# Loading the query features of the layer below four slots sooner in the two sliding-window attention backwards

## The chip, the cores and the metric

The kernel runs on one core of a Trainium2 chip. The metric is the device time of one launch in microseconds (us), lower is better. The kernel before takes 2128.89 us, the median of 3 runs (2128.79 to 2133.01). The execution that the profiler recorded took 2126.94 us.

## The reference, cut to what matters

A sequence of 2048 rows with 640 features goes forward through four residual layers, and then the gradients of the input and of the four weight matrices are computed. Layers 0 and 2 are linear attention (A), layers 1 and 3 sliding-window softmax attention (B), all with 32 heads of 20 features.

```
phi = lambda t: where(t > 0, t + 1, exp(t)) + 1e-6
A:  q, k, v = split(x @ wqkv);  pq, pk = phi(q), phi(k)
    kv = einsum("bhsd,bhse->bhde", pk, v);  z = pk.sum(s)
    o = (pq @ kv) / (pq . z + 1e-6);  return o @ wo
B:  scores = q @ k.T / sqrt(20), kept where 0 <= i - j < 256
    o = softmax(scores) @ v;  return o @ wo
x = x + A(layernorm(x));  x = x + B(layernorm(x))      (twice)
out = x;  gradients of sum(out * grad_out) in x, A_wqkv, A_wo, B_wqkv, B_wo
```

The backward of a layer A needs, for all rows, the outer product of the query features `pq` with the gradient `dn` of numerator and denominator, summed over the whole sequence. These are the outer products of the title. They need the gradient that leaves the layer B above, and the gradients of keys and values need the finished sum.

## The kernel before, in words

The 2048 rows are 16 tiles of 128 rows, and two tiles make a chunk, so that there are eight chunks, c = 0 to 7. The passes run one after the other: forward through the four layers; attention backward of layer 3; linear attention backward of layer 2; attention backward of layer 1; the rest of that one; linear attention backward of layer 0 with the weight gradients.

An attention backward (`core`, L1433) goes through 24 visits per chunk (`core_visit`, L782). In a visit TensorE (PE in the profile) makes the products `dp` and `s` for two blocks of heads, ScalarE (ACT) the exponentials `e` (L811), GpSimd (POOL) masks them by affine selects (L826, L830), VectorE (DVE) multiplies `dp` by the `e` of three visits before into `ds` (L815). The `ds` of four visits before is turned: by TensorE into a PSUM tile named `flip` (L837), copied out to `dsT` by VectorE (L844) or ScalarE (L842), or in some visits by a transposing DMA. The products of six visits before are added up (`acc`).

Between these parts each visit carries pieces of other work from a written plan. `plan_before` (L909) prepares the next chunk: it loads `gb` and `ob`, and multiplies the turned gradient by `WoTB` into PSUM tiles named `dense`. `plan_behind` (L967) takes a finished chunk on to the layer below. The start of its plan is 32 slots per chunk, two chunks after the chunk itself; a slot is three quarters of a visit, so 32 slots are 24 visits. The places of its pieces within that are the list `bh` of `PLACES` (L53), the lists `bl3` and `bl1` for the last chunk:

- `load` (`bh[26]` = 3.9): the normalized rows `hnb` and the incoming gradient `gc`, 320 KB each; they are first used by `ln` (L1059, L1062) from slot 20.2 on.
- `turn`, `store`, the products `dh`, `ln`, `ln2`, `flip`, `prod`, `fold`, `red`: what makes the gradient of the layer below and from it `dn`.
- `load_q` (`bh[31]` = 38): the query features `pqb` of the chunk's two tiles, 320 KB, into a buffer of which there is one.
- `outer` (`bh[24]` = 40.2 and `bh[25]` = 44.6): three heads' groups each of the outer products `pqb` with `dn` into a PSUM tile named `outer`, added to `macc` by VectorE (L258).

With slot 38 a chunk's `pqb` load stands behind the `hnb` and `gc` loads of the next chunk, whose plan began at slot 32 of this one, so at 35.9. In layer 1 chunk 6 has its own places for some pieces (`late`, L1019), `load_q` among them. Plans are sorted by slot and handed out to half visits (`slots`, L903).

The PSUM tiles `flip`, `dense` and `outer` take turns in two buffers. During the attention backward the order on all five engines is the order in which the program issues the work, SyncE (SP) among them, and SyncE issues every DMA of the kernel (L148): its queue is one list, in which each entry waits for its own releases before the next can go. `put` (L153) and `tick` (L161) hold some of the DMAs back by parts of a visit; the loads of `plan_behind` are issued at their slot without that.

Of the kernel before, what the change touches and what calls it, by code (L numbers as in the profile page):

```python
# [49 lines left out]
    sp=[2.6, 1.1, -2.9, -3.4, 0.6, -3.8, 0.1, 0.4, 2, 1.8, 1.1, 0.8, 3, 1, 0.9, 0.5, 1.3, 1.1, 1, 1, 1.5],  # L50
    ms=[1, -0.2, 20, 31.2, 39.5],
    bf=[1.6, 4.2, 7.7, 10, 17.8, 7.7, 9.2, 10, 14, 28.4],
    bh=[13.4, 15.6, 15.8, 16.3, 17.5, 18.5, 20.2, 22.6, 25.2, 27.8, 30, 34.4, 18.7, 21.1, 21.1, 21.6, 23.8, 24.4, 25.1, 26, 29.6, 31.8, 33.3, 35.9, 40.2, 44.6, 3.9, 7.8, 7.5, 11.6, 20.7, 38],  # L53
    bl3=[13.4, 15, 15.5, 16.2, 17.3, 17.7, 18.5, 20.2, 25.9, 28.6, 29.3, 36, 19.7, 19.9, 20.3, 22.7, 23.9, 24.8, 26.3, 26.7, 30.1, 31.8, 33.1, 36.4, 40.2, 44.6, 13.4, -5.7, -4.4, 14, 19.4, 35.1],
    bl1=[12.9, 15.1, 15.5, 16.2, 18.1, 19.6, 20.2, 22.2, 25.7, 27.8, 30.7, 34.2, 18.7, 19.4, 21.1, 21.6, 23.4, 24.3, 24.3, 25.9, 29.6, 31, 33.3, 35.3, 40.9, 45, 0.5, -4.8, -3.6, -1.2, 0.5, 1],
    la=[-10.3, -2.5, 2.1, 2.4, 1.9, 3.2, 4.6, 6.2, 7.2, 8, 4.9, 8, 8.3, 10, 11.8, 13.9, 14, 16.2, 16.9, 17, 19.2, -2.3, 3.6],
# [1674 lines left out]
```

## Time and profile before

| | |
|---|---|
| median of 3 runs | 2128.89 us |
| profiled execution | 2126.94 us |
| span in the profile, first to last instruction | 2125.2 us |
| TensorE matmul busy | 1987.4 us, 94% of the span |
| VectorE, ScalarE, GpSimd busy | 1388.1, 1300.8, 1014.0 us |
| mean granted TensorE clock | 0.988 |
| attention backward of layer 3, about 660 to 1062 us | TensorE busy 372.64 of 402 us, DMA share 0.79 |
| attention backward of layer 1, about 1224 to 1626 us | TensorE busy 370.68 of 402 us, DMA share 0.77 |

In the timelines of this document a row gives the start in us from the start of the span, the duration in us, the engine (PE matmul, PEld weight load, SPq the queue that issues DMAs), the line, the operation, what it writes and reads, how many instructions were merged into the row, and in brackets the idle time of the engine before it with what ended it. A line 204 is the helper that issues every matmul, so those are told apart by their tiles.

### The profile page before, as it was taken

To read this page: it belongs to the slowest core of one execution; us is meant where nothing else is said; L and a number is where in the kernel's file an instruction comes from. 1 tells how busy PE (TensorE), PEld (TensorE's weight loads), DVE (VectorE), ACT (ScalarE), POOL (GpSimd) and SP (SyncE) were. 2 spreads that over 40 slices of the span, in tenths; PEclk is the share of its full clock that TensorE was granted. 3 is DMA by queue.
4 is the path that set the end of the run, shared out by engine and by line. 5 is a ranking of instruction groups with operands and counts; after the bars stand their busy time and mean duration, and the time that the engine had idled before them with its cause. 6 is when DMAs were issued, how large, how long until landed. Compare 5 with 4: busy or idle time off the path is not lost.

```text
span 2125.2 us, 75617 instructions
## 1 busy us (share of the span) xinstructions
PE 1987.4 (94%) x32332; PEld 1530.7 (72%) x32332; DVE 1388.1 (65%) x2696; ACT 1300.8 (61%) x1818; POOL 1014.0 (48%) x1594
## 2 busy tenths in 40 slices
PE   8989998899988899999979988999999899999999
PEld 6667776667766777777768777777777788887644
DVE  7788886788855888888848768888886244310000
ACT  6558888478886787777747767777776244420000
POOL 1046666056665577777633356777764312220000
PEclk9999999999999999999999999999999999999999
DMA  7598886688883688888899746889887989979650
GB/s 254 202 232 226 217 214 185 202 227 220 215 218 118 174 170 188 181 190 181 172 290 263 220 110 143 184 177 206 186 178 184 311 238 271 262 206 309 225 169 19
DMA packets 667937, 432.17 MB, mean 203 GB/s; under 512 B 396880, under 2 KB 637904, under 8 KB 667344
## 3 DMA queue, kind: packets, MB, share of 16 engines
q1 hardware_dynamic: 667600, 427.34, 78.1%
q8 instruction: 252, 4.13, 0.8%
q14 instruction: 85, 0.70, 0.1%
HBM read 197.79 MB, written 147.32 MB: 162 GB/s over the span
## 4 chain that ended last, share of the span: by engine, by line
PE 53%; DVE 8%; ACT 6%; DMA 4%; issue 4%; POOL 4%; SPq 1%; DVEq 0%; POOLq 0%; ACTq 0%
PE dense L204 19%; PE wg L204 15%; DVE ds L815 5%; PE acc L204 5%; PE dp L204 3%; PE flip L225 2%; PE flip L837 2%; DMA pqb<-pqk 2%; ACT e L811 2%; PE sT L204 1%; ACT eT L469 1%; PE ops L204 1%; POOL e L830 1%; POOL e L826 1%; ACT dsT L842 1%
## 5 line engine op out<-in xcount | busy, mean ns | idle before, releaser
L815 DVE TENSOR_TENSOR ds<-dp,e 128x1024 bf16<-128x1024 f32 (+1 forms) x368 | 441.6, 1200 | 115.8 <-PE s L204 77.5
L811 ACT ACTIVATE e<-s 128x1024 bf16<-128x1024 f32 (+1 forms) x368 | 371.7, 1010 | 121.4 <-PE s L204 87.3
L469 ACT ACTIVATE eT<-sT 128x2048 bf16<-128x2048 f32 x180 | 338.3, 1879 | 94.1 <-PE sT L204 72.3
L204 PE MATMUL wg<-rhs,lhs 128*128 128x240 bf16 (+3 forms) x2720 | 370.3, 292 | 1.0 <-DMA lhs<-o 1.0
L204 PEld LDWEIGHTS <-lhs 128*128 128x128 bf16 x2720 | 250.8, 98 | 93.6 <-DMA lhs<-o 1.2
L830 POOL TENSOR_SCALAR_AFFINE_SELECT e<-e 128x256 bf16<-128x256 bf16 x448 | 182.6, 422 | 134.3 <-ACT e L811 133.4
L477 POOL TENSOR_SCALAR_AFFINE_SELECT eT<-eT 128x512 bf16<-128x512 bf16 x256 | 163.7, 643 | 113.3 <-ACT eT L469 109.2
L204 PEld LDWEIGHTS <-dqT 128*128 128x128 bf16 x1920 | 173.6, 97 | 59.4 <-issue 5.1
L826 POOL TENSOR_SCALAR_AFFINE_SELECT e<-e 128x512 bf16<-128x512 bf16 x256 | 162.8, 636 | 87.7 <-ACT e L811 82.1
L204 PE MATMUL acc<-slabqs,ds 128*128 128x20 bf16 x2880 | 193.7, 173 | 2.9 <-ACT part L896 2.4
L204 PE MATMUL acc<-ds,e 128*128 128x20 bf16 x2880 | 190.9, 172 | 0.0
L204 PEld LDWEIGHTS <-ds 128*128 128x128 bf16 x2880 | 171.6, 96 | 22.2 <-issue 17.8
L204 PE MATMUL dp<-slabT,dT 32*128 32x128 bf16 (+1 forms) x1920 | 148.0, 247 | 38.1 <-DVE ds L815 34.0
L1355 DVE CAST wr<-wg 128x240 bf16<-128x240 f32 (+3 forms) x48 | 22.8, 474 | 229.9 <-PE wg L204 221.1
L204 PEld LDWEIGHTS <-e 128*128 128x128 bf16 x2880 | 163.7, 96 | 5.2 <-issue 2.6
L204 PE MATMUL dense<-WB,hnT 128*128 128x320 bf16 x960 | 160.7, 301 | 1.2 <-ACT hnT L228 0.7
L204 PE MATMUL dense<-WTA,dqT 128*128 128x320 bf16 x960 | 156.0, 299 | 0.6 <-DVE dqT L1191 0.3
L204 PE MATMUL dense<-WTB,dqT 128*128 128x320 bf16 x960 | 152.7, 300 | 0.0
L1353 ACT CAST wr<-wg 128x240 bf16<-128x240 f32 (+3 forms) x32 | 13.2, 412 | 227.7 <-PE wg L204 213.1
L1220 POOL TENSOR_TENSOR dh<-dh,lg 128x640 f32<-128x640 f32 x31 | 44.6, 1439 | 225.7 <-DVE s L1217 225.7
L204 PE MATMUL s<-slabT,slabqT 32*128 32x128 bf16 (+1 forms) x1920 | 146.6, 248 | 4.2 <-DMA slabqT<-T 1.7
L480 POOL TENSOR_SCALAR_AFFINE_SELECT eT<-eT 128x512 bf16<-128x512 bf16 x224 | 143.3, 640 | 15.0 <-ACT eT L469 13.6
(189 smaller groups left out, 4386.6 us busy)
## 6 DMA issues: line engine op xcount, KB each, us to landing
T<-T SPq DMA_DIRECT2D x96, 256.0 KB, 3.8
s<-s SPq DMA_DIRECT2D x32, 512.0 KB, 3.3
slabT<-T SPq DMA_DIRECT2D x64, 256.0 KB, 3.7
dqkv<-dqa SPq DMA_DIRECT2D x32, 480.0 KB, 4.6
rhs<-dqkv SPq DMA_DIRECT2D x32, 480.0 KB, 6.5
rhs<-dqkv SPq DMA_DIRECT2D x16, 960.0 KB, 7.2
hn<-hn SPq DMA_DIRECT2D x64, 160.0 KB, 3.2
lpqk<-pqk SPq DMA_DIRECT2D x16, 640.0 KB, 6.4
```

Of the source, the lines that this page charges most:

```text
L204: return self.nc.tensor.matmul(out, lhsT=lhsT, rhs=rhs, start=start, stop=stop, skip_group_check=True, **kw)
L225: self.nc.tensor.transpose(t[0:w, j, :], src[:, c0:c0 + w], self.ident)
L469: nc.scalar.activation(e, s, ACT.Exp)
L477: nc.gpsimd.affine_select(out=e, in_=e, compare_op=ALU.is_ge, fill=0.0, base=0, pattern=[[0, 4], [1, P]], channel_multiplier=-1)
L480: nc.gpsimd.affine_select(out=e, in_=e, compare_op=ALU.is_ge, fill=0.0, base=-1, pattern=[[0, 4], [-1, P]], channel_multiplier=1)
L811: nc.scalar.activation(u.e[:, :, 0:w], s[:, :, 0:w], ACT.Exp)
L815: nc.vector.tensor_tensor(out=d.ds[:, :, 0:w], in0=d.dp[:, :, 0:w], in1=d.e[:, :, 0:w], op=ALU.mult)
L826: nc.gpsimd.affine_select(out=v, in_=v, pattern=[[0, 4], [1 if far else -1, P]], **kw)
L830: nc.gpsimd.affine_select(out=v, in_=v, pattern=[[0, 2], [1 if far else -1, P]], **kw)
L837: nc.tensor.transpose(ps[:, 4 * j + i, :], f.ds[:, j, i * P:(i + 1) * P], self.ident)
L1220: eng.tensor_tensor(out=x["dh"], in0=x["dh"], in1=L["g"][:, i, :], op=ALU.add)
L1355: nc.vector.tensor_copy(o[:, 0:w], ps[:, 0:w])
```

## The change

One number of the list `bh` is 34 in place of 38: the slot of `load_q` for every chunk but the last (and but chunk 6 in layer 1, which has its own place). The two lists of the last chunk stay.

```
-    bh=[13.4, 15.6, ..., 40.2, 44.6, 3.9, 7.8, 7.5, 11.6, 20.7, 38],
+    bh=[13.4, 15.6, ..., 40.2, 44.6, 3.9, 7.8, 7.5, 11.6, 20.7, 34],
```

Every engine's instructions keep their order except SyncE's. In SyncE's list twelve `pqb` loads, six in each attention backward (chunks 0 to 5), move past two entries: before, the three stood as `hnb`, `gc`, `pqb`, now as `pqb`, `hnb`, `gc`. The load of chunk 6 in layer 3 falls into the pass after the attention backward, where the order of SyncE is found by a scheduler, and keeps its place. Completion signals of DMAs go round eight semaphores by place in the list, so the three loads trade semaphores: an entry waits until the DMA eight places before it has landed, whichever it is.

More of the change, by code (lines that the diff above doesn't have):

```diff
@@ L52 @@
     bf=[1.6, 4.2, 7.7, 10, 17.8, 7.7, 9.2, 10, 14, 28.4],
-    bh=[13.4, 15.6, 15.8, 16.3, 17.5, 18.5, 20.2, 22.6, 25.2, 27.8, 30, 34.4, 18.7, 21.1, 21.1, 21.6, 23.8, 24.4, 25.1, 26, 29.6, 31.8, 33.3, 35.9, 40.2, 44.6, 3.9, 7.8, 7.5, 11.6, 20.7, 38],
+    bh=[13.4, 15.6, 15.8, 16.3, 17.5, 18.5, 20.2, 22.6, 25.2, 27.8, 30, 34.4, 18.7, 21.1, 21.1, 21.6, 23.8, 24.4, 25.1, 26, 29.6, 31.8, 33.3, 35.9, 40.2, 44.6, 3.9, 7.8, 7.5, 11.6, 20.7, 34],
     bl3=[13.4, 15, 15.5, 16.2, 17.3, 17.7, 18.5, 20.2, 25.9, 28.6, 29.3, 36, 19.7, 19.9, 20.3, 22.7, 23.9, 24.8, 26.3, 26.7, 30.1, 31.8, 33.1, 36.4, 40.2, 44.6, 13.4, -5.7, -4.4, 14, 19.4, 35.1],
```

## The prediction

> **What bounds the kernel now.** I read the page's busy times and the chain that ended last first, then the waits, then the timeline around single waits.
>
> ```profile
> PE 1987.4 (94%) x32332; PEld 1530.7 (72%) x32332; DVE 1388.1 (65%) x2696; ACT 1300.8 (61%) x1818; POOL 1014.0 (48%) x1594
> PE dense L204 19%; PE wg L204 15%; DVE ds L815 5%; PE acc L204 5%; PE dp L204 3%; PE flip L225 2%; PE flip L837 2%; DMA pqb<-pqk 2%; ACT e L811 2%; PE sT L204 1%; ACT eT L469 1%; PE ops L204 1%; POOL e L830 1%; POOL e L826 1%; ACT dsT L842 1%
> ```
>
> TensorE is the bound. The transfer `pqb<-pqk`, which the change moves, holds 2% of the chain. That share is the transfers' whole length, though, not what they cost. What TensorE stood still for them is in the waits of the whole span:
>
> ```profile
> PEld L204 <- DMA pqb<-pqk: 9.6, 10, 2.3
> POOL e L826 <- DMA gc<-in_grad_out_dram: 4.4, 4, 1.1
> ```
>
> The first row is TensorE's weight load, which comes ahead of the matmul, so it holds the whole wait. Ten of the twelve moved loads are waited for, 9.6 us in all, at most 2.3. The second row comes back among the rivals. So the change is about 9.6 us or 0.45% of the time, before anything is given back.
>
> **How much sooner the load lands.** One of the twelve places on the queue, and the list of DMA issues with median time to landing:
>
> ```profile
> 907.91 0.44 SPq L148 DMA_DIRECT2D hnb<-hn  x1
> 908.39 0.55 SPq L148 DMA_DIRECT2D gc<-in_grad_out_dram  x1
> 908.99 1.52 SPq L148 DMA_DIRECT2D pqb<-pqk  x1
> ```
>
> ```profile
> hnb<-hn SPq DMA_DIRECT2D x16, 320.0 KB, 4.9
> pqb<-pqk SPq DMA_DIRECT2D x16, 320.0 KB, 6.3
> ```
>
> Four slots are three visits, some 6.6 us, but on the queue the load passes two entries only, `hnb` and `gc`; the rest of what stood before it still does. It is issued 908.99 - 907.91 = 1.1 us sooner. It also lands faster, since two transfers of the same size no longer stand ahead of it: 6.3 us against 4.9 for the one now issued first, 1.4 us. Together 2.5 us, above the longest wait of 2.3. If only the issue counted, 1.1 us would remain, which is less than the two longest waits.
>
> **What one wait costs.** The largest wait in a full chunk (layer 3), and below it the two smallest (layer 1); TensorE's turn of `ds`, its weight load of `pqb`, VectorE's copy, TensorE's next product:
>
> ```profile
> 858.86 0.61 PE L837 MATMUL flip<-ident,ds 128*128 128x128 bf16 x8 [0.27 <-DVE ds L933]
> 861.11 0.41 PEld L204 LDWEIGHTS <-pqb 128*120 128x120 bf16 x6 [1.83 <-DMA pqb<-pqk]
> 862.11 0.84 PE L204 MATMUL dense<-WoTB,gT 128*128 128x320 bf16 x5
> ...
> 1476.80 0.61 PE L837 MATMUL flip<-ident,ds 128*128 128x128 bf16 x8 [0.28 <-DVE ds L933]
> 1477.46 0.41 PEld L204 LDWEIGHTS <-pqb 128*120 128x120 bf16 x6 [0.24 <-DMA pqb<-pqk]
> 1477.87 0.68 DVE L844 COPY dsT<-flip 128x1024 bf16<-128x1024 bf16 x1
> 1478.60 0.84 PE L204 MATMUL dense<-WoTB,gT 128*128 128x320 bf16 x5
> ...
> 1530.37 0.41 PEld L204 LDWEIGHTS <-pqb 128*120 128x120 bf16 x6 [0.18 <-DMA pqb<-pqk]
> ```
>
> From turn to `dense` it is 862.11 - 858.86 = 3.25 us with a wait of 1.83, and 1478.60 - 1476.80 = 1.80 with a wait of 0.24. The second is a floor: `dense` takes the PSUM buffer of `flip`, VectorE's copy out of it ends at 1477.87 + 0.68 = 1478.55, and `dense` starts 0.05 later. This copy is what is late next. So the wait of 1.83 is worth 3.25 - 1.80 = 1.45 us, each wait 0.38 less than its length, and the two of 0.24 and 0.18 nothing. In the last visits before the loop ends no `dense` follows, and I compare turn with turn (layer 3, then layer 1):
>
> ```profile
> 1019.98 1.03 PE L837 MATMUL flip<-ident,ds 128*128 128x128 bf16 x8
> 1021.14 0.70 PEld L204 LDWEIGHTS <-pqb 128*120 128x120 bf16 x6 [0.40 <-DMA pqb<-pqk]
> 1023.14 1.03 PE L837 MATMUL flip<-ident,ds 128*128 128x128 bf16 x8
> ...
> 1581.38 0.62 PE L837 MATMUL flip<-ident,ds 128*128 128x128 bf16 x8
> 1584.09 0.69 PEld L204 LDWEIGHTS <-pqb 128*120 128x120 bf16 x6 [2.27 <-DMA pqb<-pqk]
> 1586.08 1.03 PE L837 MATMUL flip<-ident,ds 128*128 128x128 bf16 x8
> ```
>
> 3.16 us against 4.70: the wait of 2.27 is worth 1.54, that of 0.40 I take as nothing. The other six waits are 9.6 - 1.83 - 0.24 - 0.18 - 0.40 - 2.27 = 4.7 us, less 6 x 0.38 = 2.4. The sum of the waits is 1.45 + 1.54 + 2.4 = 5.4 us; without the floor it would be 9.6, the upper bound, and nothing is the lower.
>
> **The clock.** Behind the wait of 1.83 the visit that follows ran slower than its like one chunk later; starts of `dp` in the two, and the granted clock in stretches of 3.4 us:
>
> ```profile
> 862.88 0.34 PE L204 MATMUL dp<-slabT,dT 32*128 32x256 bf16 x2
> 866.32 0.24 PE L204 MATMUL dp<-slabT,dT 32*128 32x128 bf16 x2
> ...
> 916.82 0.28 PE L204 MATMUL dp<-slabT,dT 32*128 32x256 bf16 x2
> 918.98 0.23 PE L204 MATMUL dp<-slabT,dT 32*128 32x128 bf16 x2
> ```
>
> ```profile
> 859.55:862.97 3.42, 1.85 (x39) 1.48 (x43) 1.61 (x3) 0.70 (x1) 2.95 (x5) 1.00 0.83 173
> 862.97:866.39 3.42, 3.42 (x49) 2.17 (x51) 2.31 (x3) 1.02 (x1) 1.64 (x4) 0.50 1.09 225
> ...
> 1016.57:1019.98 3.41, 2.40 (x75) 2.04 (x73) 3.35 (x4) 2.25 (x3) 1.33 (x3) 1.00 1.35 269
> 1019.98:1023.40 3.42, 3.29 (x56) 2.58 (x50) 2.38 (x4) 1.25 (x3) 1.42 (x4) 0.50 0.89 165
> ```
>
> The visit took 3.44 us instead of 2.16. TensorE was busy 1.85 of the 3.42 us that hold the wait, and the next stretch of that length has half the clock. If the half-clock stretch goes with its wait, 1.28 us more are gained. Against it: at 1019.98 half clock followed a stretch with 2.40 us busy and no long wait. I take it as going, at odds of about two to one. The Trainium skill, in TensorE: Matmul & The Clock Gate, section HAM oscillation, asks for gaps above about 3.4 us before the clock is lowered; by that rule a wait of 1.83 us would not have done it, the stretch would come from elsewhere and stay, and the sum would be the waits alone. The trace lowers the clock after a window that was only half busy, which is shorter than the rule wants.
>
> **What the change adds or delays.** No instruction and no byte is added. `hnb` and `gc` are issued one entry later, about 0.5 us, and land behind one more transfer. Their first use:
>
> ```profile
> 936.15 0.82 DVE L1059 CUSTOM_DVE_ANT_0 lna<-dh,hnb 128x640 f32<-128x640 f32 x1
> ```
>
> 936.15 is 28 us after the issue at 907.91; the delay, at most the 2.5 us that `pqb` wins, is hidden by some 20 us, and I put it at nothing. Behind the three stands a transposing DMA that still has all three ahead of it. The `pqb` buffer was last read 21 slots earlier, so the load finds it free, and it no longer stands behind ScalarE's release of `hnb`. The chunk 6 load keeps its queue place: nothing.
>
> **The sum.** 5.4 + 1.28 = 6.7 us off the profiled 2126.94, so 2120.2 there. The runs' median is 1.95 above the profiled execution, so 2128.89 - 6.7 = 2122.2. That the gain reaches the end I read from the chunks: the stretch below, a chunk that starts as one wait for `pqb` ends and has next to none at its own end, ran at a DMA share of 0.93, so the transfers can follow the faster pace.
>
> ```profile
> 1425.00:1477.00 52.00, 49.27 (x1104) 38.70 (x1105) 43.12 (x58) 40.57 (x62) 38.74 (x67) 1.00 0.93 192
> ```
>
> **The rivals.** First, the waits go and the clock does not: 5.4 us, 2123.5. Second, the gain is eaten by other late transfers, since a share of 0.93 leaves little room; if each of the ten places gave back half of its 0.67 us, 3.4 us would be left, 2125.5, within the noise. Third, the load lands little sooner, because the transfers are served side by side and only the issue counts: then the two longest waits give 1.1 us each and the others their 2.4, so 4.6 us and 2124.3, still nearly the same; only a load that wins nothing at all would give 2128.9. Fourth, on the other side: the later `gc` holds up GpSimd's masks. The second row of the waits says that a mask waited four times for `gc`, 1.1 us each. If it does, `gc` comes later by one transfer, half of the 2.5 us, in twelve places: 15 us, less the 6.7 won, so 8 us slower, 2137; it decides from 0.6 us a place on. Against it stand the two rows of that mask:
>
> ```profile
> 857.83 0.63 POOL L826 TENSOR_SCALAR_AFFINE_SELECT e<-e 128x512 bf16<-128x512 bf16 x1 [1.10 <-DMA gc<-in_grad_out_dram]
> 1475.77 0.63 POOL L826 TENSOR_SCALAR_AFFINE_SELECT e<-e 128x512 bf16<-128x512 bf16 x1 [1.10 <-ACT e L811]
> ```
>
> The same mask in the other layer idled the same 1.10 us, put down to ScalarE's `e`; it reads `e` alone, so `gc` is a coincidence in the releaser's name.
>
> **How the numbers follow.** Waits and clock: 0.45, the predicted 2122.2. Waits without clock, the first and third rival: 0.25, 2123.5 to 2124.3. Half eaten: 0.1, 2125.5. Nothing won: 0.08, 2128.9. Masks or another loss I do not see: 0.12, 2132 to 2137. About 0.2%, 4.3 us, is what a measurement of this kernel can tell from no change, so faster means below 2124.6. The first two cases lie 1 to 2.4 us from that line, and I move 0.02 of them to no change: faster 0.68, same 0.2, slower 0.12. The low end takes all 9.6 us and two more half-clock visits of 1.28: 2128.89 - 12.2 = 2116.7, taken as 2117. The high end takes in no change and 1.6 us of spread: 2130.5. The likeliest case alone reaches from 2119 to 2124.5.
>
> **What would show it.** In the changed kernel's waits the ten waits for `pqb` are gone or below 0.3 us, the share of `pqb` in the chain falls to nothing, and from turn to `dense` every full chunk shows 1.80 us, with VectorE's copy L844 ending just before `dense`. In the list of DMA issues `pqb` lands in about 4.9 us and `gc` in about 6.3. The clock row behind 862.97 shows 1.00. I am wrong if waits for `dsT`, a slab or `gc` grow by what `pqb` loses, if half-clock stretches turn up elsewhere in number, or if VectorE's copy is later than in the row I took the floor from.

## The result, and the profile after

The changed kernel takes 2125.78 us (median of 20 runs) against 2132.03 for the kernel before (20 runs beside it): a ratio of 0.9967, 95% interval 0.9954 to 0.9979. That is 0.33% faster; 0.31% was forecast. The medians lie 6.25 us apart. Two later comparisons gave 0.9969 (0.9948 to 0.9991) and 0.997 (0.9955 to 0.9985). The kernel before took 3.1 us more beside the changed one than its median of 3 runs, from which the forecast was made. So 2125.78 lies above the 2122.2 that were forecast and above the prediction's line of 2124.6 for "faster", though within its range; faster it is only against the runs beside it.

The profiled execution of the changed kernel took 2130.39 us with a span of 2128.6, longer than the profiled one before, which lay below its own median. The spans therefore say nothing here, and the places have to be looked at one by one. The first fence is the page's busy times of the changed kernel; the second is the group of weight loads of `pqb` in the list of groups (busy time, mean ns, idle time before them and what ended it).

```profile
PE 1993.5 (94%) x32332; PEld 1533.7 (72%) x32332; DVE 1387.4 (65%) x2696; ACT 1301.5 (61%) x1818; POOL 1014.2 (48%) x1594
```

```profile
L204 PEld LDWEIGHTS <-pqb 128*120 128x120 bf16 x192 | 15.3, 141 | 6.1 <-issue 4.7 <-DMA pqb<-pqk 0.2
```

Of the 9.6 us that TensorE waited for `pqb`, 0.2 are left, in one place. The issue order in one chunk of layer 3, and what TensorE does there:

```profile
860.63 0.47 SPq L148 DMA_DIRECT2D slabT<-T  x1
861.14 0.53 SPq L148 DMA_DIRECT2D pqb<-pqk  x1
861.77 1.01 SPq L148 DMA_DIRECT2D hnb<-hn  x1
```

```profile
868.18 0.61 PE L837 MATMUL flip<-ident,ds 128*128 128x128 bf16 x8 [0.28 <-DVE ds L933]
868.57 0.49 PEld L204 LDWEIGHTS <-pqb 128*120 128x120 bf16 x6
869.25 0.68 DVE L844 COPY dsT<-flip 128x1024 bf16<-128x1024 bf16 x1
869.99 0.84 PE L204 MATMUL dense<-WoTB,gT 128*128 128x320 bf16 x5 [0.19 <-DVE dsT L844]
```

The weight load no longer waits, and `dense` now waits for VectorE's copy of `flip`: from turn to `dense` 869.99 - 868.18 = 1.81 us, where the floor was put at 1.80.

To compare whole executions I took from each trace the time from one visit's first product `s` to the next. The table has the visit with the first outer product at its first four places in each layer (the full chunks), the fifth and last such visit, which no `dense` follows (headed "last chunk"), the length of the two attention backwards together from the first visit's start to the last one's, and the time in them at half clock (granted clock 0.50).

| | layer 3 | layer 1 | last chunk, 3 and 1 | both backwards, us | half clock, us |
|---|---|---|---|---|---|
| before | 3.85, 4.70, 3.47, 3.84 | 3.90, 3.96, 3.25, 3.25 | 2.94, 4.49 | 793.7 | 34.1 |
| before, second trace | 5.85, 3.65, 3.42, 3.89 | 3.25, 4.47, 3.29, 3.51 | 2.86, 4.35 | 798.6 | 37.5 |
| changed | 3.25, 3.25, 3.25, 3.45 | 3.25, 3.25, 3.25, 3.25 | 2.78, 2.77 | 793.5 | 37.5 |
| changed, second trace | 3.25, 3.25, 3.25, 3.25 | 3.25, 3.25, 3.25, 3.25 | 1.88, 2.07 | 786.8 | 17.1 |
| changed, third trace | 3.25, 3.25, 3.25, 3.53 | 3.25, 3.25, 3.25, 3.25 | 1.88, 2.73 | 790.9 | 27.3 |

The visit falls to 3.25 us in 22 of 24 places; the 3.45 holds a wait of 0.48 us for a slab, the 3.53 one of 0.7 us for `pqb`. The two backwards together go from 796.2 (mean of two) to 790.4 (mean of three), 5.8 us, but the longest after is as long as the shortest before, so the traces alone do not settle the size.

The runs say where most of the gain comes from. For each run of the two later comparisons its mean granted clock is on record, and since the traces show no clock but 1.00 and 0.50, (1 - clock) x 2 x span is its time at half clock. In the mean that goes from 65.2 to 53.5 us in the first comparison and from 68.5 to 54.5 in the second (29 runs before, 12 after in each): 11.7 and 14.0 us less, 3.4 and 4.1 stretches of 3.41 us. At the prediction's 1.28 us for one such stretch this is an estimated 4.4 and 5.3 us, of the 5.2 and 7.2 us by which the mean times differ. A straight line of time against half-clock time through the 29 runs before gives about the same price, 1.2 and 1.4 us a stretch. So the larger part of the gain is clock, and 1 to 2 us are left for the time that TensorE stood still. The split is an estimate: the price is that of one visit and of a line, and runs with longer waits may be those with more half clock.

### The profile page after: what moved, and what is told of

The parts are those of the page before. It is cut to its first block, busy times and chain, and to the rows that moved or that the text cites. A ratio compares the mean times of both kernels' runs of the same rounds, so it can differ in the third digit from the quotient of the medians.

```text
span 2128.6 us, 75619 instructions
## 1 busy us (share of the span) xinstructions
PE 1993.5 (94%) x32332; PEld 1533.7 (72%) x32332; DVE 1387.4 (65%) x2696; ACT 1301.5 (61%) x1818; POOL 1014.2 (48%) x1594
## 5 line engine op out<-in xcount | busy, mean ns | idle before, releaser
L204 PE MATMUL dp<-slabT,dT 32*128 32x128 bf16 (+1 forms) x1920 | 149.1, 248 | 38.4 <-DVE ds L815 34.1
```

The lines of the kernel that those rows point to most:

```text
L204: return self.nc.tensor.matmul(out, lhsT=lhsT, rhs=rhs, start=start, stop=stop, skip_group_check=True, **kw)
```

## The experiments

**The kernels again.** The kernel before and the changed kernel were profiled once and twice more.

> The kernel before a second time, for its trace. If its waits for pqb belong to the kernel and not to one execution, they are again 7 to 12 us in all over 9 or more places, and the visits that hold them take 3.25 us or more. Half-clock stretches in the two attention backwards: 25 us or more in sum if the waits bring them (34.2 us in the first trace, 17.0 and 37.6 in the two of the changed kernel).

> The changed kernel a second time, for its trace. Theory W (the gain is the waits for pqb less what the PSUM copy gives back, 5.4 us in all): none of the ten visits holds a wait for pqb above 0.3 us, each of the eight full ones takes 3.25 us, the time ratio is 0.9975 or a little under. Theory T (what the waits gave comes back as late transposes: the first trace of the changed kernel waited 4.7 us for dsT against 1.3 before): the waits for dsT are again above 4 us. If they were chance, they fall to 1 to 2 us.

> The changed kernel a third time, beside the kernels with the products later. Ratio 0.9965 to 0.9975, no wait for pqb above 0.3 us.

The kernel before waited 10.1 us for `pqb` in the second trace, in nine places; the changed kernel had none in its second trace and one of 0.7 us in its third, where none above 0.3 was expected. The waits belong to the kernel. A part of them comes back elsewhere. Waits for the transposed `ds`, in the waits of before (two traces) and after (three):

```profile
PEld L204 <- DMA dsT<-ds: 1.3, 2, 0.8
...
PEld L204 <- DMA dsT<-ds: 3.5, 2, 2.3
```

```profile
PEld L204 <- DMA dsT<-ds: 4.7, 4, 1.9
...
PEld L204 <- DMA dsT<-ds: 4.1, 5, 1.9
...
PEld L204 <- DMA dsT<-ds: 5.4, 7, 1.7
```

They rise from 2.4 us in the mean to 4.7, by 2.3 us, though the two traces before alone differ by 2.2. With the waits for `gb`, which go from 1.9 to 2.8, the waits of TensorE's weight loads for DMAs in the two backwards fall from 14.0 and 16.4 us to 9.6, 7.1 and 9.3: of 9.6 us less at `pqb` about 6.5 are left, and about 3 come back.

**One layer at a time.**

```
- (14 if late else A[31], load_q)
+ (14 if late else A[31] - (4 if l == 3 and not last else 0), load_q)    # second kernel: l == 1
```

> The load moves in layer 3 alone. Theory W: the waits for pqb in layer 3 go (0.98, 1.83, 0.60, 0.97, 0.40 us before), worth 2.9 us, those in layer 1 stay at 4 to 5 us in sum; ratio 0.9985 to 0.999, to 0.998 if a half-clock stretch behind a wait goes too. Theory T: the waits for dsT in layer 3 grow by 2 to 3 us, those of layer 1 do not, and the ratio is 1.000.

> The load moves in layer 1 alone. Theory W: the waits for pqb in layer 1 go (1.03, 1.09, 0.24, 0.18, 2.27 us before), worth 2.9 us, those of layer 3 stay; ratio 0.9985 to 0.999; its gain and that of the layer 3 kernel add up to that of the changed kernel. Theory T: waits for dsT grow in layer 1 alone and the ratio is 1.000.

Layer 3 alone: ratio 0.998 (0.9959 to 1.0002); layer 1 alone: 0.999 (0.9968 to 1.0013). Neither can be told from 1, and the medians, 2131.34 and 2129.06 us against 2129.97 before, show no gain at all. That the two ratios multiply to 0.997, what the changed kernel has, fits Theory W but does not show it. The waits split cleanly (layer 3 moved, then layer 1 moved):

```profile
PEld L204 <- DMA dsT<-ds: 4.5, 5, 1.5
PEld L204 <- DMA pqb<-pqk: 3.6, 5, 1.1
```

```profile
PEld L204 <- DMA pqb<-pqk: 4.0, 3, 2.6
...
PEld L204 <- DMA dsT<-ds: 1.6, 2, 0.8
```

The waits for `pqb` that remain all lie in the layer that was not moved. All 4.5 us of waits for `dsT` in the first kernel lie in layer 3, all 1.6 in the second in layer 1, as Theory T expects. But in the second trace of the kernel before 3.5 us lay in layer 3 as well, and 1.1 of the 4.5 come ahead of the first outer product, so these two traces do not show how much of it the change brings.

**Half way: between the two loads.** `gc` gets a piece of its own, and the load stands in front of it.

```
+ def load_g(): x["g"] = self.load(..., "gc", ...)        # taken out of load()
- plan = [(A[26], load), ...
+ plan = [(A[26], load), (A[26] + 0.1, load_g), ...        # and bh[31] = 35.95
```

> The load stands between hnb and gc: one place sooner instead of two. Landing by place: it is issued 0.5 us sooner and has one transfer less ahead of it, 1.2 to 1.3 us in all. Then the waits of 0.98, 0.60, 0.97, 0.40, 1.03, 1.09, 0.24, 0.18 go, and those of 1.83 and 2.27 leave 0.5 and 1.0; 0.1 and 0.6 to 0.7 of them count above the floor, so the gain is 4.6 of 5.4 us; ratio 0.998. Rival (the transfers are served side by side, so that only the issue counts): waits of about 0.5 us stay in five places, 1.3 and 1.8 in the two long ones, and the gain is 2.5 us, ratio 0.999.

```profile
PEld L204 <- DMA dsT<-ds: 4.3, 4, 1.3
...
PEld L204 <- DMA pqb<-pqk: 0.6, 2, 0.3
```

One place on the queue already takes the waits from 9.6 to 0.6 us, all eight visits stand at 3.25, and the rival that only the issue counts, with waits of 0.5 to 1.8 us left in seven places, falls. The time, 0.9987 (0.9972 to 1.0002), can be told neither from the changed kernel's nor from no change. Its runs spent 63.1 us at half clock in the mean (clock 0.9852), 5.2 us less than the kernel before on that chip (68.3): the waits are gone, the half clock mostly not. Why it stays here, and what one place and two places differ by in time, stays open.

**Sooner still: slot 30.**

> The load goes to slot 30, so that it passes the slabs and the loads of the next chunk too and stands before the last dsT transpose ahead of them. Theory W: pqb was already early enough at slot 34, so nothing more is won than there: waits for pqb 0, full visits 3.25 us, ratio 0.996 to 0.9975, the same as the changed kernel. Rival (the gain comes from the order of the loads in front of the slabs, or pqb now delays the slabs and gb): waits for gb or slabs grow and the ratio is 0.5 thousandths or more worse.

No wait for `pqb`, visits of 3.25 us, and yet the ratio is 0.9989 (0.9971 to 1.0007). The load now stands in front of `gb`, and this is what waits:

```profile
PEld L225 <- DMA gb<-in_grad_out_dram: 5.7, 5, 1.8
PEld L204 <- DMA dsT<-ds: 5.2, 7, 1.6
PEld L225 <- DMA gb<-g: 2.0, 4, 0.7
```

5.7 + 2.0 = 7.7 us for `gb`, against 2.1 in the kernel before; all waits of weight loads for DMAs in the two backwards add up to 13.4 us here, nearly what they were before (14.0 and 16.4). In the waits the rival holds: sooner is not always better on one queue, because what is overtaken is wanted as well. In time it is likely but not shown, since the intervals of the two ratios overlap. At slot 34 only `hnb` and `gc` are overtaken, which are not needed for 28 us.

**Later: slot 39.4, behind a transpose.**

> The load goes later, slot 39.4: behind the transposing DMA of ds that stood after it. That one is issued some 2.2 us after pqb was, so the load is issued 3 to 3.5 us later. Theory W: twelve waits of 3 to 5.5 us, 38 to 45 us more waiting at pqb in all, and the time grows by the same 38 to 45 us, ratio 1.018 to 1.021; above the floor one us of wait is one us of time. Rival (waits here are partly made up for by later visits, since VectorE and ScalarE use them to get ahead): the time grows by less than half of what the waits grow. Clock: if half-full windows lower the clock, a half-clock stretch follows most of these waits, 10 or more of them, and the mean granted clock falls below 0.98; by the page's rule of gaps above 3.4 us only the longest waits are followed by one.

```profile
L204 PEld LDWEIGHTS <-pqb 128*120 128x120 bf16 x192 | 15.9, 151 | 32.0 <-DMA pqb<-pqk 26.7 <-issue 4.2
```

The waits grew to 26.7 us in ten places, 17.1 more, not the 38 to 45 expected: behind the transpose the load is issued later, but with fewer transfers in front. The ratio is 1.0102 (1.0069 to 1.0134), 21.7 us, and the two backwards took 822.4 us, 26.2 more than before. So time grows by about what the waits do or more, and the rival that later visits make up for a wait falls. What comes on top is the clock: 68.3 us at half clock in the two backwards, against 34.1 and 37.5, which at 1.28 us a stretch is an estimated 12 us; 17.1 + 12 is near the 26.2. Two places of this trace, in stretches that follow the grid on which the clock changes (length, then busy time and count of PE, PEld, DVE, ACT, POOL, then the granted clock):

```profile
919.31:922.72 3.41, 1.70 (x29) 1.21 (x27) 3.12 (x5) 2.41 (x5) 2.93 (x4) 1.00 1.34 216
922.72:926.13 3.41, 2.42 (x35) 1.93 (x35) 0.55 (x1) 0.00 (x0) 1.68 (x4) 0.50 1.04 211
```

```profile
864.70:868.11 3.41, 2.20 (x42) 1.64 (x38) 3.41 (x5) 2.91 (x5) 2.43 (x4) 1.00 0.96 148
868.11:871.53 3.42, 2.46 (x50) 1.87 (x51) 1.35 (x4) 0.16 (x1) 2.18 (x4) 1.00 1.04 235
871.53:874.94 3.41, 3.08 (x82) 2.53 (x83) 3.41 (x5) 2.27 (x3) 2.32 (x5) 1.00 0.83 198
```

In the first, TensorE was busy half of a stretch and the next one has half the clock. In the second a wait of 2.07 us was cut in two by the border between two stretches, and the clock stayed. After eight of the ten waits a half-clock stretch followed or was already under way, and no wait was as long as 3.4 us at the matmul (3.3 at most). That is short of the ten expected, and the mean granted clock of this trace, 0.976, is below 0.98 as expected.

**The other side of the wait: the product two visits later.** The loads stay as they were before the change.

```
- bh=[..., 35.9, 40.2, 44.6, ...]
+ bh=[..., 35.9, 42.8, 44.6, ...]
```

> The loads stay as before, the first outer product moves from slot 40.2 to 42.8, two visits later, so that the other side of the wait moves. Theory W: pqb has landed long before, no wait is left, and the visit that held the outer product drops from 3.25 to about 2.48, as in chunks without one; the visit that takes it in grows from 1.87 by 0.4 to 0.8. Gain 5.4 us plus 0 to 0.38 a chunk, 0 to 4 us; ratio 0.9955 to 0.9975. Rival (it is the order on the DMA queue that matters, not the wait): the ratio is 1.000, since the queue inside the loop is the same.

> The kernel with the first outer product at slot 42.8 and the loads as before, once more, against the changed kernel on the same chip. By the visits of its first trace a chunk takes 51.80 us against 52.43 in the changed kernel, 6 us over the ten chunks: ratio 0.994 to 0.9955, and below that of the changed kernel. If the floor by VectorE's copy did not cost time in the end, the two are within 0.1%.

Ratios 0.9958 (0.9941 to 0.9976) and 0.9964 (0.9943 to 0.9985): at least as fast as the changed kernel, with the DMA queue of the kernel before. The rival that the order of the queue is what matters falls. The move also takes the product away from the hand-over of a PSUM buffer, so how much of this gain is the wait is seen only beside the next kernel. The visit that held the product falls to 2.49 us, the one that takes it in stays at 1.87 instead of growing by 0.4 to 0.8:

```profile
L204 PEld LDWEIGHTS <-pqb 128*120 128x120 bf16 x192 | 14.1, 132 | 7.1 <-issue 6.0
```

```profile
861.57 0.62 PE L837 MATMUL flip<-ident,ds 128*128 128x128 bf16 x8
862.61 0.41 PEld L204 LDWEIGHTS <-pqb 128*120 128x120 bf16 x6
862.63 0.53 PE L204 MATMUL outer<-dn,pqb 128*120 128x126 bf16 x6
863.75 0.49 PE L204 MATMUL outer<-dn,pqb 128*120 128x126 bf16 x6 [0.25 <-ACT dsT L842]
```

In the new visit no `dense` follows the product, so nothing stands behind a copy there; but the second product now comes 1.1 us after the first and its visit grows from 2.09 to 2.27. With the median visit at each of the 24 places, a full chunk takes 53.02 us before (52.75 in the second trace), 52.42 to 52.43 in the three traces of the changed kernel, and 51.80 here. The two backwards took 782.2 and 780.8 us. Beside the changed kernel on the same chip the runs show less than the visits: 2124.43 against 2125.91 us, within the 0.1% that was named for a floor that costs nothing in the end, and the ratio is above the 0.994 to 0.9955 expected. The waits for `dsT` are 4.2 and 5.3 us, as in the changed kernel, so the new order of the loads is not what brings them.

**Both together, and the second product moved too.**

> The changed kernel with the first outer product at slot 42.8 as well. Theory W: nothing is left to win from the load once the product is later, so this is as fast as the kernel with the late product alone, within 0.1%. If the floor by VectorE's copy (0.38 us a chunk) goes with the new place, both are up to 4 us faster than the changed kernel.

> As the kernel with the first product at slot 42.8, and the second one moves from 44.6 to 51.3 in chunks 0 to 4, away from the first. With the first product two visits later, the visit of the second had grown from 2.09 to 2.27 us. Expected: that visit back at 2.09, the one that takes the product in at 1.87 as before: 0.18 us in each of ten chunks, 1.8 us less, 0.1%, too small for the clock of the runs but plain in the visits. If it grows the visit that takes it in, nothing is won.

```
- (A[25], outer, ...)
+ (A[25] + (6.7 if c < 5 else 0), outer, ...)          # with bh[24] = 42.8, load as before
```

Load and product moved: 0.9961 (0.9945 to 0.9976), 51.80 us a chunk, 784.7 us for both backwards. With the product later the earlier load wins nothing more (0.9961 against 0.9958 with the load as before), while with the product in its old place it wins 0.3%. As closely as these intervals tell, the load gains through the wait at the product and not by its place on the queue. Second product moved too: its old visit is back at 2.09, but the new one grows from 1.87 to 2.03; 51.79 a chunk, nothing won; ratio 0.9955 (0.9935 to 0.9975), 783.6 us. Its waits for `dsT` are 2.7 us, though it waits nowhere for `pqb`: missing waits alone do not set them.

By the visits all kernels with the first product later are 0.63 us a chunk ahead of the changed kernel, 6 us over ten chunks; their four ratios (0.9955 to 0.9964) all lie below its three (0.9967 to 0.997), but the intervals overlap. By the traces they beat both kernels; by the runs they surely beat the kernel before.

## Why the prediction was right, point by point

- **The waits are the change.** Right as the cause: 9.6 and 10.1 us before, 0.2, none and 0.7 after, and once the product is moved out of the wait the earlier load wins nothing. The kernel with one place, whose waits went without a clear gain in time, stays an open end. In size the time stood still is the smaller part of what they cost; the clock below is the larger.
- **Two queue places, 2.5 us, are enough.** Right, with room: one place was enough. The medians to landing over all sixteen loads, moved or not, changed less than was said for `pqb` and `gc` (4.9 and 6.3 expected):

```profile
hnb<-hn SPq DMA_DIRECT2D x16, 320.0 KB, 5.4
pqb<-pqk SPq DMA_DIRECT2D x16, 320.0 KB, 5.2
gc<-in_grad_out_dram SPq DMA_DIRECT2D x8, 320.0 KB, 5.7
gc<-g SPq DMA_DIRECT2D x8, 320.0 KB, 5.7
```

- **The floor at 1.80 us and VectorE's copy as what is late next.** Right to 0.01 us in 22 of the 24 visits of three traces; the other two, at 1.64 and 2.09, follow a wait for a slab and hold one for `pqb`. The full chunks were put at 1.45 + 2.4 = 3.85 us, with a miscount: the prediction takes six other waits in its 4.7 us, but five are left (0.98, 0.60, 0.97, 1.03, 1.09), so they are worth 4.7 - 5 x 0.38 = 2.8, and the full chunks 4.2. Over the floor of 3.25 the first trace before adds up to just these 4.2, the second to 5.3.
- **The last chunks.** Undersized. 1.54 us was said, with layer 3's visit of 2.94 in the table taken as the floor. That visit was at half clock itself: it takes 1.88 us in the changed kernel's second and third traces. The two layers together go from 7.3 us (mean of 7.43 and 7.21) to 4.7 (mean of 5.55, 3.95, 4.61): 2.6, a part of which is clock.
- **The clock, 1.28 us.** Right in sign, and three to four times too small: by the runs' granted clock it is an estimated 4.4 and 5.3 us. The prediction counted the one stretch behind the wait of 1.83. But in the two traces before three and six half-clock stretches begin at or right behind a wait for `pqb` (at 862.97 and 1583.19; at 813.25, 1028.29 and 1594.9), and in the three traces of the changed kernel the same places hold three, none and one. Other stretches come at places without such a wait in both kernels, so that single traces of the changed kernel have 17.1 to 37.5 us. That waits bring half clock is shown by the kernel with the load later.
- **The transfers can follow.** Wrong in part: it was read from one chunk at a DMA share of 0.93. About 3 us came back as waits for `dsT` and `gb`. This is the second rival at nearly its price of 3.4. So the waits won less than the 5.4 us that were forecast, an estimated 1 to 2 us, and the clock more than its 1.28. The forecast of 6.7 us came out at 6.25 us between the medians and 7.0 by the ratio; that it fits so well is luck, since two errors cancel.
- **`gc` and the masks.** Right: the later `gc` cost nothing, and its part in the mask's wait was a coincidence in a name. In the changed kernel the same 1.1 us are put down to `hnb`, which now lands at that moment:

```profile
POOL e L826 <- DMA hnb<-hn: 1.1, 1, 1.1
```

## What to carry to other kernels

A transfer's share of the chain is its length; what it costs is the wait at its consumer, less what the next release takes back, and two places with a long and a short wait show that floor before anything is run. To this comes what the wait does to the clock, which was the larger part here: look at the granted clock of the runs, not only at one trace. On a shared queue a load should pass exactly those entries that have time: two places here took the waits away, the further ones brought others, for `gb`. And look at the consumer as well: moving the product to a visit without a PSUM hand-over cost nothing and, by the visits, won the wait and the floor.

## What the runs showed of the hardware

The clock is lowered after a stretch that is partly empty, well before a gap of 3.4 us. In the traces the clock changes only on a grid of 3.41 us. I took the full-clock stretches of that grid that lie wholly inside the two attention backwards, in fourteen traces, sorted them by TensorE's busy share, and asked whether the next stretch had half the clock:

| busy share of the stretch | stretches | followed by half clock |
|---|---|---|
| 0.8 and more | 2751 | 1 |
| 0.7 to 0.8 | 265 | 27 |
| 0.55 to 0.7 | 40 | 20 |
| below 0.55 | 33 | 33 |

None of the 81 stretches with half clock behind them holds or touches an idle gap of 3.4 us; the median of their longest gaps is 1.1 us. The rule of the Trainium skill that the prediction weighed (TensorE: Matmul & The Clock Gate, section HAM oscillation: no idle gaps above about 3.4 us) is too mild for this kernel: by it none of the 81 would have come. The measurement decides: about 1 us of idle time in one stretch is enough to be at risk, and half a stretch was always enough. In the places shown above a wait of 1.83 us that fell inside one stretch brought half clock and 1.28 us more, and one of 2.07 us that a border cut in two did not. The grid is not tied to the program: counted from the start of the span, its first border came at 2.8 and 0.9 us in the two traces of the kernel before, and at 1.3, 1.7 and 3.0 us in the three of the changed one. So the changed kernel collects 17 to 38 us of half clock in two attention backwards, and its time moves with it; runs of the kernel before ranged from 2121.25 to 2146.11 us.
